# Attention, a gated MLP and a mixer on one core: seven early gelus moved behind the last exp

## The chip, the cores and the metric

One core of one Trainium2 chip runs the whole program, in one launch. The metric is the device time of a run in microseconds (us). The kernel before took 442.62 us, the median of 3 runs (442.54 to 443.59). About 0.3% is what a measurement of this kernel can tell from no change.

Engines by the names of the profile: PE is TensorE's matmul and PEld its weight load, DVE is VectorE, ACT is ScalarE, POOL is GpSimd, SP issues nearly all DMAs. SBUF is the on-chip memory, and PSUM the one into which PE accumulates.

## The reference, cut to what matters

Three layers follow each other. All arrays are float32, with 2 batches, 12 heads, 448 rows of the sequence, 64 numbers per head (768 for all heads), and d_ff = 1024.

```
# attention
scores = q @ k.T / sqrt(64);  scores = cap * tanh(scores / cap)
attn = exp(scores - max) / (sum(exp(scores - max)) + 1e-9);  x = attn @ v

# the gated layer: the change is here
h = gelu(x @ w_in)                      # the tanh form of gelu
u, v = h[..., :512], h[..., 512:]
v_n = (v - mean(v)) / sqrt(var(v) + 1e-6) * g_ln
x = x + (u * (w_sg @ v_n + b_sg)) @ w_out

# the mixer
u = x + (relu(x.T @ w_tok1) @ w_tok2).T
out = u + relu(u @ w_ch1) @ w_ch2
```

## The kernel before, in words

**Attention** runs in twelve steps, one for each pair of heads (pairs 0 to 5 are batch 0, pairs 6 to 11 batch 1). For a pair, PE makes the scores of three blocks of 128 keys, each for both heads, and of the last 64 keys (L540, L655). ACT takes the tanh out of PSUM (L514) and the exp in place (L522). PE then multiplies the weights with the values (L572 for the three blocks, L561 for the last 64 keys), and DVE divides by the sums and splits the result into a high and a low part, `x` (L592 to L616, L351, L367). The step of pair n on PE holds the scores of pair n and the values of pair n-1. Scores lie in PSUM buffers `sc`, values in `gm`, of which there are four.

**Nearly all matrix products** are three matmuls on a high and a low part of each operand (`three`, recorded at L274). The weights arrive as 64-bit numbers. For w_in of v, one ACT pass (L396) and three DVE passes (L438, L449) make a float32 of them, and for the others (w_in of u, w_sg apart, w_out and the mixer's) three ACT passes (L396, L407, L420) and one of DVE (L427). Then the tile is split: cast to the high part, subtraction for the low. The raw tile `r` has two buffers.

**The early units.** When pair 5 is done, x of batch 0 is whole. Its three v units (128 rows each of x @ w_in for v, 18 matmuls of 512 columns) and four u units (128 columns each of u, 18 matmuls of 448) are interleaved with the attention of batch 1. Each ends in a gelu that ACT reads from the unit's `gm` buffer (L768); a v unit goes on with mean and variance on DVE (L814 to L816), a power on POOL (L821), the scaling (L827) and a split into `vn`. After attention come the v units of batch 1, one unit `vr` for the last 64 rows of both batches, the u units of batch 1, then the products with w_sg (`sg_unit`, 11 matmuls each), with w_out, and the mixer.

**The order** is not written out. `Plan` holds every operation with its engines, an estimated duration, a key and what it depends on; `schedule` (L128) repeatedly takes, for each engine, the operation that can start first (the key breaks ties), and the order it finds is emitted engine by engine. The program on the chip keeps this order on every engine and waits only for data and buffers. A dependency that is only in the plan moves instructions and adds no wait. gelu's function is in another table of ACT than tanh and exp, so each change between them is an `ACT_TABLE_LOAD`.

Of the kernel before, what the change touches and what calls it, by code (L numbers as in the profile page):

```python
# [12 lines left out]
AF = mybir.ActivationFunctionType  # L13
# [3 lines left out]
B, H, S, D = 2, 12, 448, 64  # L17
NP = H // 2
DM = H * D
ND = DM // 128  # L20
DF = 512
NF = DF // 128
ST = 112
NS = S // ST
NR = 3
# [197 lines left out]
class Net:  # L223
    def __init__(self, tc, io, pool, ps, anycap=False):
        self.tc, self.nc, self.io, self.pool, self.ps, self.anycap = tc, tc.nc, io, pool, ps, anycap
        self.plan = Plan()
        self.key = 0.0


    def buf(self, tag, shape, dtype=F32):  # L230
# [143 lines left out]
        self.cast(n, hi, src, r, w, key, on or {"ACT": 0}, psum)  # L374
        self.rest(n, lo, src, hi, list(r) + list(w), w, key, rest, psum)

    def weight(self, src, n, key, name):

        nc = self.nc
        rows = src.shape[0]  # L380
        out = self.buf("q" if name in ("wsg", "tok2") else "a", [rows, 2, n], F32R)
        t = self.buf("t", [rows, n], F32 if src.dtype == F32 else I32)
        if src.dtype == F32:
            self.load(rows * n * 4, lambda: nc.sync.dma_start(out=t.ap, in_=src), [t], key=key - 4)
            f = lambda: t.ap
        else:
            raw = self.buf("r", [rows, n, 2], I32)
            self.load(
                rows * n * 8,
                lambda: nc.sync.dma_start(out=raw.ap.rearrange("p n t -> p (n t)"), in_=src.bitcast(I32)),  # L390
                [raw],
                key=key - 4,
            )
            self.act(
                n,
                lambda: nc.scalar.activation(  # L396
                    raw[:, :, 1].bitcast(F32), raw[:, :, 1].bitcast(F32), AF.Copy, scale=2.0**-112
                ),
                [raw],
                [raw],  # L400
                key=key,
            )
            if name in HALVES:

                self.act(
                    n,
                    lambda: nc.scalar.activation(  # L407
                        t.ap.bitcast(U16)[:, 0::2],
                        raw.ap.rearrange("p n t -> p (n t)").bitcast(U16)[:, 1::4],
                        AF.Copy,  # L410
                        scale=2.0**-13,
                        bias=2.0**-14 - 0.5,
                    ),
                    [raw],
                    [t],
                    key=key,
                )
                self.act(
                    n,
                    lambda: nc.scalar.activation(t.ap.bitcast(F16)[:, 1::2], raw[:, :, 1].bitcast(F32), AF.Copy),  # L420
                    [raw],
                    [t],
                    key=key,
                )
                self.dve(
                    n,
                    lambda: nc.vector.scalar_tensor_tensor(  # L427
                        out=t.ap, in0=raw[:, :, 1], scalar=3, in1=t.ap, op0=ALU.logical_shift_left, op1=ALU.bitwise_or
                    ),
                    [raw, t],  # L430
                    [t],
                    key=key,
                    port=True,
                )
            else:
                self.dve(
                    n,
                    lambda: nc.vector.tensor_scalar(  # L438
                        t.ap, raw[:, :, 1], 0x0FFFFFFF, 3, ALU.bitwise_and, ALU.logical_shift_left
                    ),  # L440
                    [raw],
                    [t],
                    fast=2,
                    key=key,
                )
                for half, scalar, op in ((1, -0x80000000, ALU.bitwise_and), (0, 29, ALU.logical_shift_right)):
                    self.dve(
                        n,
                        lambda half=half, scalar=scalar, op=op: nc.vector.scalar_tensor_tensor(  # L449
                            out=t.ap, in0=raw[:, :, half], scalar=scalar, in1=t.ap, op0=op, op1=ALU.bitwise_or  # L450
                        ),
                        [raw, t],
                        [t],
                        key=key,
                        port=True,
                    )
            f = lambda: t.ap.bitcast(F32)
        self.split(n, lambda: out[:, 0], lambda: out[:, 1], f, [t], [out], key, *W_ON[name])
        return out
# [49 lines left out]
    def weigh(self, sc, nn, te, key, dt=0.2):  # L509

        nc = self.nc
        self.act(
            nn * S,
            lambda: nc.scalar.activation(te.ap, sc[:, 0:nn, :S], AF.Tanh, scale=self.qs),  # L514
            [sc, self.cb],
            [te],
            60,
            key,
        )
        self.act(  # L520
            nn * S,
            lambda: nc.scalar.activation(te.ap, te.ap, AF.Exp, scale=self.acap),  # L522
            [te, self.cb],
            [te],
            190,
            key + dt,
        )
# [236 lines left out]
        return x  # L764


    def gelu(self, out, ps, n):
        self.act(n, lambda: self.nc.scalar.activation(out.ap, ps[:, :n], AF.Gelu_apprx_tanh), [ps], [out], 60)  # L768

    def pack(self, x):  # L770

# [25 lines left out]
                psum=psum,  # L797
            )

    def v_unit(self, x, win, si):  # L800

        nc = self.nc
        ps = self.bank()
        cs = slice(0, 128) if si is None else slice(si * 128, (si + 1) * 128)
        terms = []
        for d in range(ND):
            terms += self.three(lambda i, d=d: x[d][:, i, cs], lambda i, d=d: win[d][:, i], [x[d], win[d]])
        self.mm(ps, lambda: ps.ap, terms, 512 / 448)
        v = self.h([128, 512])
        self.gelu(v, ps, 512)  # L810
        st, mv = self.buf("sm", [128, 16]), self.buf("sm", [128, 16])

        def stats():
            nc.vector.bn_stats(out=st[:, 0:6], in_=v.ap)  # L814
            nc.vector.bn_aggr(out=mv[:, 0:2], in_=st[:, 0:6])
            nc.vector.tensor_scalar(mv[:, 1:2], mv[:, 1:2], 1e-6, None, ALU.add)  # L816

        self.dve(800, stats, [v], [st, mv])
        self.gps(
            1700,  # L820
            lambda: nc.gpsimd.tensor_tensor(out=mv[:, 1:2], in0=mv[:, 1:2], in1=self.mhalf, op=ALU.pow),  # L821
            [mv],
            [mv],
        )
        self.dve(
            512,
            lambda: nc.vector.tensor_scalar(v.ap, v.ap, mv[:, 0:1], mv[:, 1:2], ALU.subtract, ALU.mult),  # L827
            [v, mv],
            [v],
            2,  # L830
        )
        vn = self.a([128, 2, 512], F32R)
        if si is None:
            self.halves(512, lambda b, p: vn[p, b], lambda p: v[p], [v], [vn, vn])
        else:
            self.split(512, lambda: vn[:, 0], lambda: vn[:, 1], lambda: v.ap, [v], [vn])
        return vn

    def u_unit(self, x, win, f):
        ps = self.bank()  # L840
        cs = slice(f * 128, (f + 1) * 128)
        terms = []
        for d in range(ND):
            terms += self.three(lambda i, d=d: win[d][:, i, cs], lambda i, d=d: x[d][:, i], [x[d], win[d]])
        self.mm(ps, lambda: ps[:, :S], terms, 1)
        u = self.h([128, S])
        self.gelu(u, ps, S)
        return u

    def sg_unit(self, b, vn, vr, wsg, u, f):  # L850
        nc = self.nc
# [174 lines left out]
    def run(self):  # L1026
        io = self.io
        self.consts()
        rows = lambda t, i, r, c0, n: io[t][i * r : (i + 1) * r, c0 : c0 + n]
        wk = lambda name, k, i: k + KEYS[name][0] + i * KEYS[name][1]  # L1030
        xs = [self.attention_anycap(n) for n in range(B * NP)] if self.anycap else self.attention_all()
        x = [xs[:NP], xs[NP:]]
        k = 10.0 * B * NP + (90 if self.anycap else 13)
        win_v = [self.weight(rows("w_in", d, 128, DF, DF), DF, wk("win_v", 0, d), "win_v") for d in range(ND)]
        win_u = [self.weight(rows("w_in", d, 128, 0, DF), DF, wk("win_u", 0, d), "win_u") for d in range(ND)]

        def stage(units, step):
            nonlocal k
            out = []
            for u in units:  # L1040
                self.key = k
                out.append(u())
                k += step
            return out

        vn, u, g, x2, tr, h1, U = ([None] * B for _ in range(7))
        early, k = (k, k - 70) if self.anycap else (k, EARLY)
        vn[0] = stage([lambda s=s: self.v_unit(x[0], win_v, s) for s in range(NR)], 6.5)
        u[0] = stage([lambda f=f: self.u_unit(x[0], win_u, f) for f in range(NF)], 6.5)
        k = early  # L1050
        vn[1] = stage([lambda s=s: self.v_unit(x[1], win_v, s) for s in range(NR)], 4)
        self.key = k
        xp = self.pack(x)
# [8 lines left out]
        for b in range(B):  # L1062
# [3 lines left out]
            k = kk  # L1066
# [115 lines left out]
```

## Time and profile before

| what | value |
| --- | --- |
| time, median of 3 runs | 442.62 us |
| profiled execution, its own time | 444.11 us |
| span of its trace | 442.3 us |
| mean granted PE clock, share of full | 0.991 |
| PE busy | 427.0 us (97%) |
| ACT busy | 265.7 us (60%) |
| DVE busy | 264.8 us (60%) |
| POOL busy | 105.5 us (24%) |

The profiled execution took 444.11 us, of which the span, from the first instruction to the last, is 442.3 us; 1.81 us lie outside. Its shares are means over stages: from about 40 us to the end of attention at 144.2 us ACT is busy nearly all the time, and after that PE works without a break while ACT has room. So a stretch of the trace tells more than the whole. In the profile, "T idle before, releaser" gives what ended an engine's wait; a matmul's record includes its way through the array, so records of matmuls that follow each other overlap, and the distance between two starts is the better measure of what PE spent.

### The profile page before, as it was taken

How to read it: one execution, taken by the hardware profiler on the slowest of the kernel's cores; microseconds unless marked ns; L12 is line 12 of the kernel's file. 1: busy time of each engine (PE TensorE's matmuls, PEld its weight loads, DVE VectorE, ACT ScalarE, POOL GpSimd, SP SyncE). 2: the span in 40 equal slices, each digit the busy share in tenths (PEclk: the TensorE clock that was granted, in tenths of full speed). 3: DMA queues.
4: the chain of work that ended last, by engine and by line, in shares of the span. 5: the costliest groups of instructions: out<-in, count | busy, mean ns of one | idle time of the engine just before them, and what ended most of it. 6: DMA issues, size and time to landing. Idle time of an engine off the chain costs nothing.

```text
span 442.3 us, 5467 instructions
## 1 busy us (share of the span) xinstructions
PE 427.0 (97%) x2050; PEld 350.2 (79%) x2050; DVE 264.8 (60%) x413; ACT 265.7 (60%) x386; POOL 105.5 (24%) x105
## 2 busy tenths in 40 slices
PE   8997989998999999999999999999999999999994
PEld 5553546566775889999999999999999999999993
DVE  4899989776665765896546899655202242344210
ACT  6998899999999567525537825775404333353100
POOL 0333342320100141567005473111010011011100
PEclk9999989999999999999999999999999999999998
DMA  7535546352120402202402105444201223533010
GB/s 266 207 125 173 176 128 210 102 157 88 47 70 2 142 5 92 83 1 99 139 1 96 48 1 168 164 144 142 96 0 49 96 90 116 184 117 123 34 44 29
DMA packets 14867, 44.84 MB, mean 101 GB/s; under 512 B 1904, under 2 KB 4208, under 8 KB 14832
## 3 DMA queue, kind: packets, MB, share of 16 engines
q1 hardware_dynamic: 14688, 44.30, 30.4%
q8 instruction: 18, 0.29, 0.3%
q14 instruction: 17, 0.14, 0.1%
q10 hardware_dynamic: 144, 0.11, 0.1%
HBM read 41.65 MB, written 2.75 MB: 100 GB/s over the span
## 4 chain that ended last, share of the span: by engine, by line
PE 78%; ACT 12%; DVE 7%; issue 2%; POOL 0%; DVEq 0%; POOLq 0%; ACTq 0%
PE gm L274 48%; PE sc L274 20%; PE gm L572 5%; ACT a L514 3%; ACT a L522 3%; PE sc L540 2%; DVE t L449 1%; DVE q L367 1%; PE sc L905 1%; ACT L768 1%; DVE t L438 1%; DVE h L592 1%; PE gm L561 1%; PE sc L342 1%; DVE h L616 1%
## 5 line engine op out<-in xcount | busy, mean ns | idle before, releaser
L274 PE MATMUL gm<-a,a 128*128 128x448 f32 (+1 forms) x556 | 115.2, 363 | 0.0
L274 PEld LDWEIGHTS gm<-a,a 128*128 128x128 f32 x556 | 102.8, 188 | 8.4
L274 PE MATMUL sc<-x,a 128*128 128x448 f32 x432 | 89.4, 368 | 0.0
L274 PEld LDWEIGHTS sc<-x,a 128*128 128x128 f32 x432 | 81.1, 188 | 8.2
L572 PE MATMUL gm<-a,v 128*128 128x448 f32 x144 | 61.8, 558 | 4.8 <-ACT a L522 2.8
L427 DVE SCALAR_TENSOR_TENSOR t<-r,t 128x512 int32<-128x512 int32 (+1 forms) x52 | 40.5, 782 | 30.1 <-ACT t L420 27.9
L274 PE MATMUL gm<-q,a 128*128 128x448 f32 x268 | 57.3, 367 | 0.0
L407 ACT ACTIVATE t<-r 128x512 uint16<-128x512 uint16 (+1 forms) x52 | 40.5, 784 | 25.3 <-DVE a L367 20.8
L396 ACT ACTIVATE r<-r 128x512 f32<-128x512 f32 (+1 forms) x58 | 38.9, 670 | 25.3 <-DMA r<-ch_in 23.1
L274 PEld LDWEIGHTS gm<-q,a 128*128 128x128 f32 x268 | 50.3, 188 | 4.7
L572 PEld LDWEIGHTS gm<-a,v 128*128 128x128 f32 x144 | 25.5, 191 | 29.6 <-issue 20.6
L368 POOL TENSOR_TENSOR a<-t,a 128x512 fp32r<-128x512 f32 x21 | 29.4, 1402 | 77.6 <-DVE a L351 73.7
L355 POOL TENSOR_SCALAR a<-t 128x512 fp32r<-128x512 f32 x19 | 12.2, 644 | 127.3 <-PE gm L274 71.9
L420 ACT ACTIVATE t<-r 128x512 f16<-128x512 f32 (+1 forms) x52 | 40.3, 774 | 0.0
L367 DVE TENSOR_TENSOR a<-t,a 128x512 fp32r<-128x512 f32 x35 | 24.6, 704 | 20.7 <-POOL a L355 20.1
L522 ACT ACTIVATE a<-a,acap 128x896 f32<-128x896 f32 x36 | 36.5, 1043 | 0.1
L514 ACT ACTIVATE a<-sc,qs 128x896 f32<-128x896 f32 x36 | 35.1, 1004 | 2.2 <-PE sc L540 2.2
L891 POOL TENSOR_TENSOR h<-x 128x448 f32<-128x448 f32 (+1 forms) x25 | 33.5, 1368 | 9.0 <-PE gm L274 6.1
L274 PE MATMUL gm<-x,a 128*128 128x448 f32 x144 | 31.0, 372 | 0.0
L938 DVE SCALAR_TENSOR_TENSOR a<-sc,a 128x896 fp32r<-128x896 f32 x9 | 9.8, 1092 | 33.3 <-ACT a L935 33.3
L274 PEld LDWEIGHTS gm<-x,a 128*128 128x128 f32 x144 | 27.1, 188 | 3.3 <-issue 1.0
L935 ACT ACTIVATE a<-sc 128x896 fp32r<-128x896 f32 x9 | 8.3, 920 | 32.7 <-PE sc L274 32.7
(97 smaller groups left out, 492.5 us busy)
## 6 DMA issues: line engine op xcount, KB each, us to landing
r<-ch_in SPq DMA_DIRECT2D x36, 512.0 KB, 3.3
r<-w_in_in SPq DMA_DIRECT2D x12, 512.0 KB, 3.9
q<-qk_in SPq DMA_DIRECT2D x11, 544.0 KB, 4.3
v<-va_in SPq DMA_DIRECT2D x12, 288.0 KB, 4.4
r<-w_out_in SPq DMA_DIRECT2D x6, 512.0 KB, 3.4
out_t<-h SPq DMA_DIRECT2D x11, 224.0 KB, 1.9
r<-tok_in SPq DMA_DIRECT2D x2, 512.0 KB, 3.4
t<-w_sg_in SPq DMA_DIRECT2D x4, 224.0 KB, 2.5
```

The lines of the kernel that those rows point to most:

```text
L274: self.nc.tensor.matmul(view(), l, rr, start=(i + m == 0), stop=(i + m == n - 1))
L355: lambda: nc.gpsimd.tensor_scalar(out(), src(), 1.0, 0.0, ALU.mult, ALU.add),
L367: "DVE": ("DVE", n / 0.96 + 155, lambda: nc.vector.tensor_tensor(**args()), not psum),
L368: "POOL": ("POOL", n * 2.3 + 60, lambda: nc.gpsimd.tensor_tensor(**args()), True),
L396: lambda: nc.scalar.activation(raw[:, :, 1].bitcast(F32), raw[:, :, 1].bitcast(F32), AF.Copy, scale=2.0**-112),
L407: lambda: nc.scalar.activation(t.ap.bitcast(U16)[:, 0::2], raw.ap.rearrange("p n t -> p (n t)").bitcast(U16)[:, 1::4], AF.Copy, scale=2.0* ...
L420: lambda: nc.scalar.activation(t.ap.bitcast(F16)[:, 1::2], raw[:, :, 1].bitcast(F32), AF.Copy),
L427: lambda: nc.vector.scalar_tensor_tensor(out=t.ap, in0=raw[:, :, 1], scalar=3, in1=t.ap, op0=ALU.logical_shift_left, op1=ALU.bitwise_or),
L514: lambda: nc.scalar.activation(te.ap, sc[:, 0:nn, :S], AF.Tanh, scale=self.qs),
L522: lambda: nc.scalar.activation(te.ap, te.ap, AF.Exp, scale=self.acap),
L572: nc.tensor.matmul(A[h][:, :S], V[:, 3 * j + h : 3 * j + h + 2].rearrange("p c d -> p (c d)"), E[j][:, h], start=(j == 0), stop=(j == 2),)
L891: lambda: self.nc.gpsimd.tensor_tensor(out=out.ap, in0=parts(0), in1=parts(1), op=ALU.add),
```

## The change

The gelu of an early unit no longer stands behind its matmuls. The unit's sums are copied out of PSUM by ACT or DVE, whichever the plan finds free: for v into a buffer `a`, for u into the buffer that holds u afterwards. The gelu, and for v all that follows it, is recorded later, and gelu operations depend in the plan on the last exp, so all fifteen stand behind the whole of attention. The loads of w_in of u depend in the plan on the last exp of the pair with number 6, the seventh pair. The estimate of a gelu's fixed part goes from 60 to 100 ns. The branch of the program for a large cap (`anycap`) keeps its order.

```diff
+        self.last_exp = None
+        self.exps = {}
...
-    def weight(self, src, n, key, name):
+    def weight(self, src, n, key, name, after=None):
...
-            self.load(
+            o = self.load(
                 rows * n * 8,
...
                 key=key - 4,
             )
+            if after:
+
+                o.deps.append(after)
...
-        self.act(
+        self.last_exp = self.exps[int(key // 10)] = self.act(
             nn * S,
             lambda: nc.scalar.activation(te.ap, te.ap, AF.Exp, scale=self.acap),
...
-    def gelu(self, out, ps, n):
-        self.act(n, lambda: self.nc.scalar.activation(out.ap, ps[:, :n], AF.Gelu_apprx_tanh), [ps], [out], 60)
+    def gelu(self, out, src, n):
+        o = self.act(n, lambda: self.nc.scalar.activation(out.ap, src[:, :n], AF.Gelu_apprx_tanh), [src], [out], 100)
+        if self.last_exp:
+
+            o.deps.append(self.last_exp)
...
-    def v_unit(self, x, win, si):
+    def v_unit(self, x, win, si, late=None):
...
         self.mm(ps, lambda: ps.ap, terms, 512 / 448)
+        if late is None:
+            return self.v_rest(ps, si)
+        raw = self.a([128, 512])
+        self.cast(512, lambda: raw.ap, lambda: ps.ap, [ps], [raw], on={"ACT": 0, "DVE": 0}, psum=True)
+        return lambda: self.v_rest(raw, si)
+
+    def v_rest(self, src, si):
+        nc = self.nc
         v = self.h([128, 512])
-        self.gelu(v, ps, 512)
+        self.gelu(v, src, 512)
...
-    def u_unit(self, x, win, f):
+    def u_unit(self, x, win, f, late=None):
...
         u = self.h([128, S])
-        self.gelu(u, ps, S)
-        return u
+        if late is None:
+            self.gelu(u, ps, S)
+            return u
+        self.cast(S, lambda: u.ap, lambda: ps[:, :S], [ps], [u], on={"ACT": 0, "DVE": 0}, psum=True)
+        return lambda: (self.gelu(u, u, S), u)[1]
...
-        win_u = [self.weight(rows("w_in", d, 128, 0, DF), DF, wk("win_u", 0, d), "win_u") for d in range(ND)]
+        win_u = [self.weight(rows("w_in", d, 128, 0, DF), DF, wk("win_u", 0, d), "win_u", self.exps.get(6)) for d in range(ND)]
...
-        vn[0] = stage([lambda s=s: self.v_unit(x[0], win_v, s) for s in range(NR)], 6.5)
-        u[0] = stage([lambda f=f: self.u_unit(x[0], win_u, f) for f in range(NF)], 6.5)
+        late = None if self.anycap else 1
+        vn[0] = stage([lambda s=s: self.v_unit(x[0], win_v, s, late) for s in range(NR)], 6.5)
+        u[0] = stage([lambda f=f: self.u_unit(x[0], win_u, f, late) for f in range(NF)], 6.5)
         k = early
+        if late:
+            self.key = k + 2
+            vn[0] = [f() for f in vn[0]]
+            u[0] = [f() for f in u[0]]
```

On ACT around the scores of pair 8, two gelus of v stand between tables before (L768 is the gelu, `a_889` and `a_893` hold weights of pair 8):

```order
L768 ACT_TABLE_LOAD
L768 ACTIVATE h_877<-gm_817 128x512
L407 ACTIVATE t_880<-r_807 128x512
L514 ACTIVATE a_889<-sc_859,qs 128x896
L514 ACTIVATE a_893<-sc_860,qs 128x896
L350 CAST x_898<-h_875 128x448
L522 ACT_TABLE_LOAD
L522 ACTIVATE a_889<-a_889,acap 128x896
L522 ACTIVATE a_893<-a_893,acap 128x896
L350 CAST a_925<-h_877 128x512
```

and the same place now (L519 is tanh, L527 exp, L401, L412 and L425 are the three passes over a tile of w_in of u, L352 is the copy out of PSUM):

```order
L352 COPY a_845<-gm_788 128x512
L519 ACTIVATE a_851<-sc_829,qs 128x896
L401 ACTIVATE r_810<-r_810 128x512
L519 ACTIVATE a_864<-sc_830,qs 128x896
L412 ACTIVATE t_868<-r_810 128x512
L527 ACTIVATE a_851<-a_851,acap 128x896
L425 ACTIVATE t_868<-r_810 128x512
L527 ACTIVATE a_864<-a_864,acap 128x896
L401 ACTIVATE r_853<-r_853 128x512
L519 ACTIVATE a_899<-sc_872,qs 128x896
L412 ACTIVATE t_916<-r_853 128x512
```

The two table loads and the gelu went; a copy and seven conversion passes of w_in of u, which stood further ahead before, came in.

On ACT at the end of attention, before (`h_1308` is the last exp):

```order
L768 ACT_TABLE_LOAD
L768 ACTIVATE h_1294<-gm_1259 128x448
L514 ACTIVATE a_1300<-sc_1281,qs 128x896
L514 ACTIVATE h_1308<-sc_1296,qs 128x448
L522 ACT_TABLE_LOAD
L522 ACTIVATE a_1300<-a_1300,acap 128x896
L522 ACTIVATE h_1308<-h_1308,acap 128x448
L407 ACTIVATE t_1318<-r_979 128x512
L407 ACTIVATE t_1325<-r_1235 128x512
L420 ACTIVATE t_1318<-r_979 128x512
L350 CAST a_1336<-t_1209 128x512
```

and now (`h_1278` is the last exp, L773 the gelu):

```order
L527 ACTIVATE a_1270<-a_1270,acap 128x896
L527 ACTIVATE h_1278<-h_1278,acap 128x448
L412 ACTIVATE t_1288<-r_1013 128x512
L773 ACT_TABLE_LOAD
L773 ACTIVATE h_1295<-a_776 128x512
L773 ACTIVATE h_1048<-h_1048 128x448
L773 ACTIVATE h_1305<-a_845 128x512
L773 ACTIVATE h_1107<-h_1107 128x448
L773 ACTIVATE h_1317<-a_968 128x512
L773 ACTIVATE h_1185<-h_1185 128x448
L773 ACTIVATE h_1264<-h_1264 128x448
L425 ACTIVATE t_1288<-r_1013 128x512
```

One table load and all seven early gelus now follow the last exp.

On SP, the loads of w_in of u, `r` from `w_in_in`, stand among those of q, k (`q`) and v (`v`), before:

```order
L390 DMA r_501<-w_in_in 128x1024
L503 DMA v_507<-va_in 128x576
L478 DMA q_570<-qk_in 128x1088
L503 DMA v_584<-va_in 128x576
L390 DMA r_613<-w_in_in 128x1024
L390 DMA r_646<-w_in_in 128x1024
L478 DMA q_676<-qk_in 128x1088
L503 DMA v_687<-va_in 128x576
L390 DMA r_709<-w_in_in 128x1024
L478 DMA q_765<-qk_in 128x1088
L390 DMA r_769<-w_in_in 128x1024
L390 DMA r_807<-w_in_in 128x1024
```

and now:

```order
L483 DMA q_657<-qk_in 128x1088
L392 DMA r_663<-w_in_in 128x1024
L392 DMA r_665<-w_in_in 128x1024
L508 DMA v_674<-va_in 128x576
L483 DMA q_739<-qk_in 128x1088
L392 DMA r_774<-w_in_in 128x1024
L508 DMA v_796<-va_in 128x576
L392 DMA r_810<-w_in_in 128x1024
L392 DMA r_853<-w_in_in 128x1024
L483 DMA q_892<-qk_in 128x1088
L392 DMA r_910<-w_in_in 128x1024
```

The first of six comes two pairs' worth of other loads later, behind the q and k of pair 8 (`q_657`), and the last behind those of pair 10 (`q_892`). On PE the order of pairs and units is the same but for details: two v units with pair 7, one with pair 8, two u units with pair 9, and one each with pairs 10 and 11, all seven ahead of the last values of attention.

## Rows read from the trace of the kernel before

**Rows 1.** View of the chain that ended last: share of the span by engine.

```profile
PE 78%; ACT 12%; DVE 7%; issue 2%; POOL 0%; DVEq 0%; POOLq 0%; ACTq 0%
```

**Rows 2.** View by stretches: length, busy time and count per engine, PE clock, DMA.

```profile
52.72:61.84 9.12, 7.16 (x28) 3.55 (x26) 8.89 (x14) 8.55 (x13) 4.35 (x4) 1.00 0.50 151
61.84:65.39 3.55, 3.54 (x15) 2.14 (x15) 2.40 (x5) 3.55 (x6) 0.67 (x1) 0.62 0.44 148
65.39:102.70 37.31, 35.10 (x155) 22.55 (x154) 30.35 (x55) 35.64 (x46) 10.11 (x12) 0.99 0.48 152
102.70:144.20 41.50, 41.01 (x190) 28.05 (x188) 25.36 (x47) 40.31 (x49) 3.63 (x4) 1.00 0.15 46
144.20:177.20 33.00, 33.00 (x155) 28.82 (x154) 22.35 (x42) 21.14 (x34) 7.89 (x9) 1.00 0.26 82
177.20:200.00 22.80, 22.80 (x115) 21.13 (x114) 21.15 (x28) 8.66 (x16) 13.43 (x9) 1.00 0.12 39
```

**Rows 3.** Timeline of PE, 55 to 144 us: start, busy time, line, output<-inputs, count, idle.

```profile
55.82 0.47 PE L540 MATMUL sc<-q 64*128 64x448 f32 x2
...
61.84 1.07 PE L572 MATMUL gm<-a,v 128*128 128x448 f32 x2 [1.42 <-ACT a L522]
...
68.17 0.47 PE L540 MATMUL sc<-q 64*128 64x448 f32 x2
...
83.28 0.47 PE L540 MATMUL sc<-q 64*128 64x448 f32 x2
...
96.96 0.47 PE L540 MATMUL sc<-q 64*128 64x448 f32 x2
...
100.72 2.52 PE L572 MATMUL gm<-a,v 128*128 128x448 f32 x6 [1.32 <-ACT h L768]
...
114.28 0.47 PE L540 MATMUL sc<-q 64*128 64x448 f32 x2
...
121.02 3.81 PE L274 MATMUL gm<-x,a 128*128 128x448 f32 x18
...
124.67 1.66 PE L572 MATMUL gm<-a,v 128*128 128x448 f32 x4
...
126.27 0.48 PE L540 MATMUL sc<-q 64*128 64x448 f32 x2
...
136.68 4.67 PE L572 MATMUL gm<-a,v 128*128 128x448 f32 x12
...
144.20 12.75 PE L274 MATMUL gm<-a,x 128*128 128x512 f32 x54
```

**Rows 4.** Timeline of ACT, 128 to 133 us: a change of tables between tanh and exp.

```profile
128.30 1.90 ACT L514 ACTIVATE a<-sc,qs 128x896 f32<-128x896 f32 x2
130.22 1.28 ACT L522 ACT_TABLE_LOAD   x1
131.52 1.98 ACT L522 ACTIVATE a<-a,acap 128x896 f32<-128x896 f32 x2
```

**Rows 5.** View by lines, whole span: ACT and DVE; count, busy us, mean ns, idle before.

```profile
L768 ACT ACT_TABLE_LOAD x8 | 10.3, 1283 | 0.8 <-PE gm L274 0.7
...
L522 ACT ACT_TABLE_LOAD x7 | 9.0, 1283 | 0.1
...
L768 ACT ACTIVATE h<-gm 128x448 f32<-128x448 f32 (+1 forms) x15 | 8.5, 570 | 7.7 <-PE gm L274 7.6
...
L407 ACT ACTIVATE t<-r 128x512 uint16<-128x512 uint16 (+1 forms) x52 | 40.5, 784 | 25.3 <-DVE a L367 20.8 <-DVE big L1089 4.4
...
L883 DVE TENSOR_TENSOR h<-gm,h 128x448 f32<-128x448 f32 x12 | 7.5, 622 | 8.4 <-PE gm L274 8.3
...
L814 DVE BATCH_NORM_STATS2 sm<-h 128x6 f32<-128x512 f32 x7 | 4.8, 693 | 7.7 <-ACT h L768 7.7
...
L827 DVE TENSOR_SCALAR h<-h,sm 128x512 f32<-128x512 f32 x7 | 4.5, 661 | 0.0
```

**Rows 6.** View of DMA issues: KB each, median us from issue to landing.

```profile
r<-w_in_in SPq DMA_DIRECT2D x12, 512.0 KB, 3.9
```

## The prediction

> **What bounds the kernel now.** I read the chain of waits first: PE holds 78% of it, ACT 12%, DVE 7% [rows 1]. The stretches then say where the 12% lie. From 144.2 us on PE is busy in every microsecond (33.00 of 33.00, then 22.80 of 22.80) while ACT works 21.14 and 8.66 [rows 2]: no ACT time saved there shortens anything. In the four stretches of attention from 52.72 to 144.2 us (91.48 us together) ACT is busy for 8.55 + 3.55 + 35.64 + 40.31 = 88.05 us, and PE shows 1.96 + 0.01 + 2.21 + 0.49 = 4.67 us without a record [rows 2]. So both engines are nearly full there, and the question is which of them gives way when ACT gets lighter. The order on ACT is the same in both kernels up to the first pass over w_in of u, which falls into the step before 55.82, so what comes earlier stays as it is.
>
> The timeline of PE answers it. A step of attention starts with the first of the L540 matmuls of a pair; steps 6 to 11 start at 55.82, 68.17, 83.28, 96.96, 114.28 and 126.27, and attention ends at 144.20 [rows 3]. Step 10 is the cleanest: 11.99 us, in which one u unit takes 124.67 - 121.02 = 3.65 us. What is left, 8.34 us, is what PE needs for a pair alone. A v unit is a third of the 54 matmuls after 144.20, 12.75 / 3 = 4.25 us; a value matmul (L572) is 4.67 / 12 = 0.39 us [rows 3]. With these I set each step against what PE needs for its contents:
> - step 6, a pair alone: 12.35 us against 8.34, 4.0 lost;
> - step 7, two v units, four value matmuls fewer: 15.11 against 8.34 - 1.56 + 8.5 = 15.3, nothing lost;
> - step 8, one v unit: 13.68 against 12.6, 1.1 lost;
> - step 9, two u units: 17.32 against 15.64, 1.7 lost;
> - step 10: the measure itself, 0;
> - step 11, one u unit and the last values (twelve more L572, and six L561 that I put at 0.7 us): 17.93 against 17.4, 0.5 lost.
>
> Together 7.3 us: the most that the change can win before 144.2 us, whatever it takes off ACT. Part of the loss is seen directly: the 4.67 us without a record, and the stretch from 61.84 to 65.39, where the granted clock was 0.62 on average (part of it at 1.2 instead of 2.4 GHz), 3.55 x 0.38 = 1.35 us. The other 1.3 us lie in waits hidden under overlapping records.
>
> **The change part by part.**
>
> Tables. Seven loads before a gelu and seven before the next exp go from attention (fourteen of the fifteen on L768 and L522 [rows 5]; the load for the gelu after attention stays, a little earlier). Each takes 1283 ns, and the neighbours adjoin it: a tanh ends at 130.20, the load runs from 130.22 to 131.50, the exp starts at 131.52 [rows 4]. That is 14 x 1.29 = 18.1 us of ACT. (The Trainium skill, "ScalarE: Activation LUTs", section "What ACT_TABLE_LOAD costs", adds a drain of about 1.38 us to each load, 2.66 us for a switch. By it 14 x 2.66 = 37 us would leave ACT, an estimate. The trace shows 0.02 us between load and exp, no such drain, and the row decides.)
>
> Gelu and copies. Seven gelus of 0.57 us [rows 5], 4.0 us, leave attention, and with them the casts of three normalised v tiles, which I price like a gelu, 0.6 us each. Seven copies out of PSUM come in, four on ACT and three on DVE by the order. No copy out of PSUM of this shape is in the trace. Its nearest rows are the gelu itself, which reads the same buffer (0.57), and DVE's addition from PSUM (0.62) [rows 5]; I take 0.6, so 2.4 us on ACT and 1.8 on DVE. The ends: a copy may find its engine free, and then the `gm` buffer comes free after 0.6 us instead of 1.28 + 0.6, a gain of 1.3 each; or it stands behind a 1 us exp, and nothing is gained. On balance ACT's 88.05 us become 88.05 - 18.1 - 4.0 - 1.8 + 2.4 = 66.5, so ACT is no longer the bound between 55 and 144 us; PE is.
>
> DVE loses mean, variance, scaling and split of three v units in attention, and gains the copies and two or three casts: 30.35 of 37.31 and 25.36 of 41.50 us before [rows 2], so about equal, and not the bound.
>
> Passes over w_in of u. Their number stays, 18 on ACT (L407 is 0.78 us [rows 5], and I take no more than that for the other two) and 6 each of L427, cast and subtraction. They leave steps 5 to 8, where they were spread, for steps 7 to 9. Step 6 gains most: the two idle times I can name there, 1.42 us before 61.84 and the half clock that followed, both stood behind ACT [rows 3]. Step 7 takes it back: by the order ACT does there two pairs of tanh and exp besides three tiles and a copy, about 13 us, inside PE's 15.3; step 8 has about 11.8 inside 12.6. So the passes are covered by the units' own matmuls, with 0.8 us to spare in step 8.
>
> What is then late next, by step: 6 runs with nothing but a pair, so latency between PE, ACT and DVE shows, 0.8; 7, 0.3; 8, 0.6 for the small margin; 9, 0.4, with the wait for the gelu before 100.72 (1.32 us [rows 3]) turned into one for a copy; 10, 0; 11, 0.3, with one table load less ahead of the last exp. Sum 2.4, so 7.3 - 2.4 = 4.9 us are won by the end of attention. The ends of this term: none of the 2.4 remains (7.3 won), or all the losses but the half clock and the waits on gelu remain (2.7 won).
>
> After attention. A table load and seven gelus (1.28 + 7 x 0.6 = 5.5 us) now follow the last exp on ACT, and behind them wait the passes over w_out and w_tok1 and the gelus of batch 1's v units, whose `gm` buffers the u units need. ACT has 33.00 - 21.14 = 11.9 us of idle time up to 177.2, and the first gelu of batch 1 can't start before its 18 matmuls end, 8 us or more after 144.2, so this is covered. On DVE three units' statistics (0.69 for L814 [rows 5] and 0.3 for the two short ones), scaling (0.66) and split (priced like the scaling, 0.7) come in, 2.4 each, 7 us: 22.35 + 7 = 29.4 of 33.00. That fits, narrowly, and the next stretch had DVE at 21.15 of 22.80 already. I charge 0.1 us. If that cover is gone, rival C prices it.
>
> Forecast: 7.3 - 2.4 - 0.1 = 4.8 us. The profiled execution took 444.11 us (442.3 of span and 1.81 around it) and would come to 439.3; it was 1.5 us above the median of the runs, and a time taken now is set against that median: 442.62 - 4.8 = 437.8 us.
>
> **The rivals.**
>
> A, PE runs without any wait from step 6 on: 442.62 - 7.3 = 435.3. For it: step 10 did so with ACT busy nearly all of the time. Against it: steps 8 and 9 wait on three engines in turn, and DVE is busier than in step 10.
>
> B, slower: the tiles of w_in of u come late for the u units. With two `r` buffers a load waits until the tile two before it is combined; it lands 3.9 us after its issue [rows 6], and three ACT passes of up to 0.78 us follow, among tanh and exp in ACT's order. The sixth load stands on SP behind the q and k of pair 10. If load and passes of one tile, 3.9 + 3 x 0.78 = 6.2 us, lie bare before the first u unit, PE stands, and the half clock that followed the idle time of 1.42 us before comes back (1.35): 437.8 + 7.6 = 445.4. It decides from 4.8 us of bare wait on. For it: the passes start about 20 us later than before, and u units don't start later. Against it: by the order the sixth tile is ready 6 to 7 us into step 9, and its six matmuls stand at about 7.5 us there.
>
> The Trainium skill ("TensorE: Matmul & The Clock Gate", section on PSUM-queue depth-cycling) says that short idle times between groups of matmuls, while PSUM banks are cycled, are enough for the clock to drop again and again. Seven copies now stand between unit and bank. By that rule five such places at 1.35 us would cost 6.7 us, and the time would be 437.8 + 6.7 = 444.5, an estimate, on B's side. The trace doesn't bear it out: the stretch with the 1.32 us wait on a bank before 100.72 and that before 144.2 kept 0.99 and 1.00 [rows 2].
>
> C, given back: DVE enters the products with w_sg late, since 29.4 of 33 us leaves 3.6 for all its own waits. Once it is more than the four `gm` buffers behind, PE waits. Half of the 7 us added would be 3.5, less what the buffers hold (about 0.5): 437.8 + 3.0 = 440.8. Against it: the plan put fewer weight passes there, and those can wait.
>
> **How the numbers follow.** The forecast (437.8, its own range 435.8 to 440) has a chance of 0.60, A (435.3) 0.14, C (440.8) 0.14, B (444 to 446) 0.12. The range from 434.6 to 441.6 holds all of the first three and leaves out B and little more. About 0.3%, 1.3 us, is what a measurement of this kernel can tell from no change: faster means below 441.3. The forecast and A lie there with nearly all of their 0.74, C with a third of its 0.14: 0.78. Same is the rest of C and a little of B: 0.10. Slower is B: 0.12.
>
> **What would show it.** Right: no table load between 55 us and the last exp; attention's last value matmul some 5 us earlier, step 6 near 9 us, step 7 unchanged; ACT near 66 us busy over the same steps; PE without a gap after attention; no clock below 1.00 near 60 us. Wrong: a PE wait on a cast or L427 of w_in at the first u unit (B); PE waiting on DVE between the u units of batch 1 and w_out (C); a step 6 still over 11 us would say that ACT wasn't what held it.

## The result and the profile after

| kernel | median, us | runs, us |
| --- | --- | --- |
| before, on the same chip | 442.98 | 442.54 to 443.59 |
| after | 437.12 | 436.68 to 437.26 |

The ratio is 0.9865 [0.9848, 0.9882], so 5.86 us were won (5.2 to 6.7 by the interval); the forecast was 4.8 us and 437.8. The profiled execution of after took 437.02 us with a span of 435.1, against 444.11 and 442.3: 7.1 us. The trace thus shows 1.2 us more than the medians do, and the further profiles of before below say why. Two of the executions of before told below are far off the others, one of 699.11 us (granted clock 0.559) in before_again, which its ratio leaves out, and the profiled one of before_third, 653.48 us (0.37 on average from 300 us on), of which only the first 300 us, at 1.00, are read.

The share of the engines in the chain that ended last, in after, answers to [rows 1]:

```profile
PE 90%; DVE 6%; ACT 3%; issue 1%; POOL 0%; DVEq 0%; POOLq 0%
```

ACT fell from 12% to 3%. The stretches of after by steps 6 to 11 and the two behind attention (columns as in [rows 2]):

```profile
55.58:63.94 8.36, 8.36 (x41) 4.82 (x40) 8.16 (x14) 8.33 (x12) 5.06 (x6) 1.00 0.30 89
63.94:79.79 15.85, 15.85 (x74) 11.15 (x73) 14.76 (x25) 13.66 (x20) 3.88 (x3) 1.00 0.61 201
79.79:92.28 12.49, 12.49 (x59) 8.16 (x58) 10.42 (x19) 11.48 (x16) 2.13 (x2) 1.00 0.56 160
92.28:107.95 15.67, 15.67 (x76) 11.56 (x76) 11.61 (x21) 10.43 (x14) 1.35 (x3) 1.00 0.52 173
107.95:120.02 12.07, 12.07 (x60) 8.16 (x59) 6.98 (x13) 9.31 (x12) 0.95 (x1) 1.00 0.07 19
120.02:137.05 17.03, 17.03 (x76) 10.86 (x76) 11.46 (x24) 12.30 (x17) 1.79 (x2) 1.00 0.09 33
137.05:170.00 32.95, 32.95 (x155) 28.75 (x154) 25.18 (x55) 20.55 (x37) 8.11 (x12) 1.00 0.18 65
170.00:193.00 23.00, 23.00 (x115) 21.32 (x114) 20.75 (x26) 10.28 (x19) 13.58 (x10) 1.00 0.13 43
```

PE's busy time equals the length in every row: it has no idle time in any of them, and the clock is 1.00 in all. ACT sums to 65.51 us of the 81.47 us of the six steps; only in step 6 is it still full. (The 88.05 us of the prediction begin 3.10 us ahead of step 6; with the same 3.10 us of after, where ACT is busy for 1.96, its sum is 67.47.) Against the prediction's price for PE alone (a pair 8.34, a v unit 4.25, a u unit 3.65):

| step | before [rows 3] | after | price of what after has in it |
| --- | --- | --- | --- |
| 6 | 12.35 | 8.36 | 8.34 |
| 7 | 15.11 | 15.85 | 8.34 + 8.5 - 2 x 0.39 = 16.06 |
| 8 | 13.68 | 12.49 | 12.59 |
| 9 | 17.32 | 15.67 | 15.64 |
| 10 | 11.99 | 12.07 | 11.99 |
| 11 | 17.93 | 17.03 | 17.4 |

Step 7 is longer by 0.74 because two value matmuls moved into it from step 5 (8 of them stood in step 7 of before, 10 do now; step 5 became 0.74 shorter, 7.62 against 8.36). Attention ends at 137.05 instead of 144.20, 7.15 us earlier, and from there to the last instruction both kernels take 298.1 us.

The timeline of PE in after (columns as in [rows 3]), at the first u unit, the end of step 9, and the end of attention:

```profile
96.47 2.94 PE L276 MATMUL gm<-x,a 128*128 128x448 f32 x12
...
100.76 1.50 PE L276 MATMUL gm<-x,a 128*128 128x448 f32 x6
...
103.88 4.15 PE L276 MATMUL gm<-x,a 128*128 128x448 f32 x18
107.95 0.47 PE L545 MATMUL sc<-q 64*128 64x448 f32 x2
...
135.79 1.77 PE L577 MATMUL gm<-a,v 128*128 128x448 f32 x4
137.05 12.78 PE L276 MATMUL gm<-a,x 128*128 128x512 f32 x54
```

No row here names a wait. The first u unit began with twelve matmuls at 96.47 and went on with six at 100.76; at this place before had the wait of 1.32 us for a gelu [rows 3]. All waits of PE that the trace of after shows between 30 and 430 us (engine, tile and line, what released it: us in total, times, longest):

```profile
PE gm L577 <- ACT a L527: 1.2, 1, 1.2
PE sc L545 <- DVE q L369: 1.1, 1, 1.1
```

Both lie in step 4, ahead of everything that the change moved:

```profile
39.06 0.67 PE L545 MATMUL sc<-q,q 64*128 64x448 f32 x4 [1.14 <-DVE q L369]
...
43.16 0.99 PE L577 MATMUL gm<-a,v 128*128 128x448 f32 x2 [1.19 <-ACT a L527]
```

ACT in after, at the end of attention, answers to [rows 4]:

```profile
132.06 0.66 ACT L527 ACTIVATE h<-h,acap 128x448 f32<-128x448 f32 x1
132.62 0.77 ACT L412 ACTIVATE t<-r 128x512 uint16<-128x512 uint16 x1
133.39 1.28 ACT L773 ACT_TABLE_LOAD   x1
134.69 0.63 ACT L773 ACTIVATE h<-a 128x512 f32<-128x512 f32 x1
```

It is the one table load left beside that at the start of the program, and the seven late gelus follow it, the first at 134.69, while PE still has attention's last values to do. The copies out of PSUM, which before didn't have (groups by line and shape; count, busy us, mean ns, idle before):

```profile
L353 DVE COPY h<-gm 128x448 f32<-128x448 f32 x2 | 1.2, 625 | 0.5 <-PE gm L276 0.5
...
L352 ACT COPY a<-gm 128x512 f32<-128x512 f32 x2 | 1.2, 587 | 1.3 <-PE gm L276 1.3
L352 ACT COPY h<-gm 128x448 f32<-128x448 f32 x2 | 1.1, 534 | 6.6 <-PE gm L276 6.6
L353 DVE COPY a<-gm 128x512 f32<-128x512 f32 x1 | 0.7, 693 | 0.0
```

Four on ACT, three on DVE, 0.53 to 0.69 us each; 0.6 was assumed.

### The profile page after: what moved, and what is told of

Same layout as the page of the kernel before. It is cut to its first block, busy times and chain, and to the rows that moved or that the text cites. A ratio compares the mean times of both kernels' runs of the same rounds, so it can differ in the third digit from the quotient of the medians.

```text
span 435.1 us, 5461 instructions
## 1 busy us (share of the span) xinstructions
PE 424.8 (98%) x2050; PEld 350.4 (81%) x2050; DVE 267.3 (61%) x422; ACT 248.2 (57%) x375; POOL 99.8 (23%) x100
## 4 chain that ended last, share of the span: by engine, by line
PE 90%; DVE 6%; ACT 3%; issue 1%; POOL 0%; DVEq 0%; POOLq 0%
PE gm L276 52%; PE sc L276 21%; PE gm L577 9%; PE sc L545 4%; PE gm L566 1%; DVE t L454 1%; PE sc L660 1%; DVE q L369 1%; ACT a L519 1%; PE sc L925 1%; ACT a L527 1%; DVE t L443 1%; PE sc L344 1%; DVE h L621 1%; DVE h L597 0%
## 5 line engine op out<-in xcount | busy, mean ns | idle before, releaser
L577 PE MATMUL gm<-a,v 128*128 128x448 f32 x144 | 60.6, 553 | 1.6 <-ACT a L527 1.6
L412 ACT ACTIVATE t<-r 128x512 uint16<-128x512 uint16 (+1 forms) x52 | 40.8, 784 | 24.8 <-DVE a L369 20.5
L401 ACT ACTIVATE r<-r 128x512 f32<-128x512 f32 (+1 forms) x58 | 38.9, 671 | 24.8 <-DMA r<-ch_in 22.2
L370 POOL TENSOR_TENSOR a<-t,a 128x512 fp32r<-128x512 f32 x19 | 25.8, 1359 | 77.7 <-DVE a L353 59.0
L425 ACT ACTIVATE t<-r 128x512 f16<-128x512 f32 (+1 forms) x52 | 40.2, 774 | 0.0
L369 DVE TENSOR_TENSOR a<-t,a 128x512 fp32r<-128x512 f32 x37 | 26.0, 706 | 21.6 <-POOL a L357 20.1
L357 POOL TENSOR_SCALAR a<-t 128x512 fp32r<-128x512 f32 x18 | 11.1, 619 | 119.7 <-PE gm L276 72.0
L519 ACT ACTIVATE a<-sc,qs 128x896 f32<-128x896 f32 x36 | 35.0, 1004 | 5.3 <-PE sc L545 5.3
L527 ACT ACTIVATE a<-a,acap 128x896 f32<-128x896 f32 x36 | 36.5, 1043 | 0.1
```

Of the source, the lines that this page charges most:

```text
L369: "DVE": ("DVE", n / 0.96 + 155, lambda: nc.vector.tensor_tensor(**args()), not psum),
L370: "POOL": ("POOL", n * 2.3 + 60, lambda: nc.gpsimd.tensor_tensor(**args()), True),
L401: lambda: nc.scalar.activation(raw[:, :, 1].bitcast(F32), raw[:, :, 1].bitcast(F32), AF.Copy, scale=2.0**-112),
L412: lambda: nc.scalar.activation(t.ap.bitcast(U16)[:, 0::2], raw.ap.rearrange("p n t -> p (n t)").bitcast(U16)[:, 1::4], AF.Copy, scale=2.0* ...
L577: nc.tensor.matmul(A[h][:, :S], V[:, 3 * j + h : 3 * j + h + 2].rearrange("p c d -> p (c d)"), E[j][:, h], start=(j == 0), stop=(j == 2),)
```

## The experiments

The theory: PE's waits in steps 6, 8, 9 and 11 were the cost, ACT caused them, and each part of the change frees the steps in which its own instructions stood. (The trace of before puts two of these waits down to DVE, 0.61 us in step 8 and 0.19 in step 11, and one to POOL, 0.30 in step 11; same_table tests whether these too hung on ACT.) The readings set against it are named in each expectation. Medians are compared with runs of before on the same chip (443.58 us for the first four kernels, 443.36 for the next four).

**before_again**: the kernel before, unchanged, for the spread and a second profile.

> The kernel before, profiled once more. If the stretch at the half clock near 62 us belongs to every execution, the profile shows it again and the times stay within 0.3% of 443. If it belongs to some executions only (my theory, since the profiled one took 444.1 and the others 442.5 to 443.6), a profile without it has a span near 441 and step 6 near 11 us instead of 12.4; the spread of the times, about 1.3 us, is then this stretch.

443.57 us, ratio 0.9998 [0.9984, 1.0012]. Step 6 took 12.38 us. In its profile the stretch behind the wait of step 6 is again slow (columns as in [rows 2]):

```profile
61.80:65.60 3.80, 3.73 (x14) 2.11 (x14) 2.47 (x5) 3.80 (x7) 0.67 (x1) 0.59 0.48 138
```

**before_third**, the same kernel, for a third look at that stretch:

> One more look at the kernel before. Both profiles of it so far hold a stretch at the half clock in step 6 (12.35 and 12.38 us), while two kernels with the same two waits in step 6 kept the full clock (10.85 us). If the drop hangs on the waits alone, step 6 is 12.4 again; if it comes in some executions only, step 6 may be near 10.9 with the time near 442.1.

Its first 300 us are at full clock, and step 6 took 9.90 us there, with one wait of 1.28 us where the two profiles above have waits of 0.54 and 1.42, or 0.56 and 1.42, and no drop of the clock:

```profile
0.00:300.00 300.00, 291.35 (x1403) 227.91 (x1404) 223.13 (x356) 223.62 (x325) 91.65 (x85) 1.00 0.34 110
300.00:650.00 350.00, 345.45 (x649) 281.82 (x647) 39.94 (x57) 42.09 (x61) 13.78 (x20) 0.37 0.10 33
```

So it is no test of what follows the same two waits.

**before_fourth**, the same kernel again. (The expectation takes the 0.661 of before_third for its whole span; by the rows just shown it was 1.00 up to 300 us.)

> The same look once more, since the one before ran at a clock of 0.661 throughout. Drop tied to the waits: step 6 at 12.4 us. Drop in some executions only: step 6 at 10.9 us and a time near 442.1.

443.61 us in one run, beside 442.58 for before on that chip: not near 442.1, although step 6 took 10.86 us, so the total of one execution doesn't tell whether the drop was there. The timeline of PE from the start of step 6, with the starts of step 7 (67.16) and of what follows attention (143.48), and, below it, the stretch of before_fourth:

```profile
56.30 0.47 PE L540 MATMUL sc<-q 64*128 64x448 f32 x2
...
60.05 0.47 PE L655 MATMUL sc<-q 128*128 128x448 f32 x1 [0.55 <-ACT a L514]
...
62.34 1.02 PE L572 MATMUL gm<-a,v 128*128 128x448 f32 x2 [1.42 <-ACT a L522]
...
67.16 0.47 PE L540 MATMUL sc<-q 64*128 64x448 f32 x2
...
143.48 6.87 PE L274 MATMUL gm<-a,x 128*128 128x512 f32 x28
```

```profile
61.80:65.60 3.80, 3.26 (x17) 1.87 (x18) 3.62 (x7) 3.80 (x7) 0.67 (x1) 1.00 0.44 144
```

The wait of 1.42 us is the one of [rows 3], and the clock stayed at 1.00. So a wait of 1.28 to 1.42 us stands in step 6 of all four profiles of before, and the half clock behind it in two of them; it costs about 12.35 - 10.86 = 1.5 us there. Attention ends at 144.20, 144.21, 142.06 and 143.48 in the four (before, before_again, before_third, before_fourth), so after ends it 7.15, 7.16, 5.01 and 6.43 us earlier; the medians show 5.86 above and 6.31 below.

**gelu_late_only**: the gelus behind attention, w_in of u where it was.

```diff
-  win_u = [self.weight(..., "win_u", self.exps.get(6)) for d in range(ND)]
+  win_u = [self.weight(..., "win_u") for d in range(ND)]
```

> One part alone: gelu of the early units behind attention, w_in of u converted where it was before. Theory 1 (PE's waits end step by step, each edit frees its own steps): step 6, which holds no table load but six or seven passes over w_in of u, stays 2.5 to 4 us above PE's 8.3; steps 8, 9 and 11 go to PE's own time, 3.3 us won, so 439.5. Theory 2 (only the 22 us taken off ACT count, wherever they lie): all is won here, 437.1. Theory 3 (the moved passes carry the gain): nothing won, 442.6.

439.53 us, ratio 0.9912 [0.9891, 0.9933], as theory 1 had it (439.5). Its steps 6, 8 and 9:

```profile
56.34:67.19 10.85, 8.89 (x42) 4.62 (x41) 10.51 (x17) 10.85 (x17) 5.09 (x6) 1.00 0.50 158
...
82.38:94.88 12.50, 12.50 (x60) 8.21 (x59) 9.80 (x19) 10.21 (x14) 2.09 (x2) 1.00 0.57 193
94.88:110.50 15.62, 15.62 (x76) 11.54 (x76) 6.84 (x13) 9.58 (x12) 1.73 (x2) 1.00 0.18 56
```

Steps 8 and 9 are those of after to 0.05 us, and step 11 is (17.05). Step 6 keeps the waits of before, 0.55 and 1.41 us, with ACT busy in all of its 10.85 us: the passes over w_in of u still stand in it. DVE is busy for 10.51 us there too, but ACT has no idle time in which it could have waited for DVE.

**same_table**: before, with tanh in place of gelu in the seven early units. tanh is in the table that exp uses, so the 14 loads go; in the two traces every engine otherwise has the same instructions in the same order. This kernel leaves out the gelu of the seven early units.

```diff
-  def gelu(self, out, ps, n):
+  def gelu(self, out, ps, n, early=False):
+      fn = AF.Tanh if early else AF.Gelu_apprx_tanh
```

> The kernel before in its own order on every engine, but the seven early units take tanh instead of gelu (so the computation is another there), which needs no change of tables: fourteen loads go, and nothing else moves. Theory 1: step 6 unchanged, steps 8, 9 and 11 at PE's own time: 3.3 us won, 439.5. Theory 2: 18 of 22 us go from ACT, so nearly all of the gain, 437.5 to 438. If table loads are no matter at all: 442.6.

439.58 us, ratio 0.9919 [0.9900, 0.9937], the same as gelu_late_only. Steps 6, 8 and 9:

```profile
55.93:66.78 10.85, 8.89 (x41) 4.63 (x41) 10.52 (x17) 10.85 (x17) 5.07 (x6) 1.00 0.50 149
...
81.96:94.45 12.49, 12.49 (x59) 8.16 (x59) 11.26 (x20) 11.00 (x15) 3.12 (x4) 1.00 0.42 137
94.45:110.07 15.62, 15.62 (x76) 11.54 (x76) 10.89 (x20) 10.88 (x15) 2.27 (x3) 1.00 0.32 100
```

The table loads alone carry the whole of what the gelu part of the change brings. Where the gelu itself stands, the copies, and the new estimate of a gelu are worth nothing that these runs can tell. No wait of PE is left behind step 6, so those that the trace of before puts down to DVE and POOL hung on ACT's loads as well. Fourteen loads of 1.29 us, 18.1 us of ACT, bought 4.0 us.

**winu_late_only**: w_in of u behind the seventh pair, gelu where it was.

```diff
-  late = None if self.anycap else 1
+  late = None
   # and gelu() as before, with no dependency on the last exp
```

> The other part alone: w_in of u loaded and converted behind the seventh pair, gelu where it was. Theory 1: step 6 falls to about 8.5 us (2.5 to 4 us won), but its passes now join fourteen table loads in steps 7 to 11, where ACT was busy 73 of 76 us; they add about 4 us there, so in sum -3 + 4: 443.5, between 442 and 445. Theory 2 (sum on ACT): nothing leaves ACT, 442.6. Theory 3 (the moved passes carry the gain): 438 to 439.

442.56 us (12 runs), ratio 0.9978 [0.9966, 0.9990]. Its steps 6 to 9, and two of the waits of PE in steps 8 and 9:

```profile
55.55:63.90 8.35, 8.35 (x42) 4.82 (x41) 8.15 (x14) 8.32 (x12) 5.03 (x6) 1.00 0.30 87
63.90:79.76 15.86, 15.86 (x74) 11.16 (x73) 13.80 (x25) 14.76 (x20) 2.60 (x3) 1.00 0.63 212
79.76:94.08 14.32, 12.73 (x58) 8.09 (x57) 10.46 (x22) 14.26 (x20) 2.77 (x3) 1.00 0.38 108
94.08:112.69 18.61, 16.39 (x78) 11.38 (x77) 14.30 (x28) 18.49 (x25) 3.36 (x4) 1.00 0.49 161
```

```profile
83.79 2.52 PE L577 MATMUL gm<-a,v 128*128 128x448 f32 x6 [1.58 <-ACT h L773]
...
99.02 1.40 PE L577 MATMUL gm<-a,v 128*128 128x448 f32 x3 [1.52 <-ACT h L773]
```

The time alone doesn't decide: theory 1 had expected 443.5, and 442.56 is theory 2's number. The steps do. Step 6 is that of after (8.35). But steps 8 and 9 became 0.64 and 1.29 us longer than before: ACT is busy for 14.26 of 14.32 and 18.49 of 18.61 us, since the passes came on top of tables and gelus, and PE waits for the gelus (and, in step 9, 0.70 us for DVE). The two parts alone bring 4.05 and 1.02 us, 5.1 together; the whole change brings 5.9 and 6.3 (the first result and the next run). Between medians, with their intervals, that difference is at the edge of what can be told. The steps show it plainly: with the passes in them, the tables and gelus cost steps 8 and 9 14.32 - 12.49 and 18.61 - 15.67, 4.8 us together; with the passes further ahead it was 1.2 + 1.7 = 2.9 in before. The passes moved from step 6 lie under PE's work only where the table loads have gone.

**after_again**: the kernel after, with the next three.

> The changed kernel once more, beside the same runs of the kernel before as the next three. Theory 1 (PE's waits in steps 6, 8, 9 and 11 were the whole cost): 437.2, a ratio near 0.986. Of the 7.2 us between the two profiles, 1.4 is the half clock of step 6, which executions of the kernel before have or haven't; if most of them have it, the ratio is nearer 0.985, if few have it, nearer 0.987.

437.05 us, ratio 0.9853 [0.9833, 0.9874]; step lengths as in the table above to 0.02 us.

**extra_act**: after, with nine needless ACT passes of 224 columns in each of steps 9 to 11.

```diff
+  for _ in range(EXTRA if 9 <= n else 0):      # EXTRA = 9
+      o = self.act(224, lambda: nc.scalar.activation(self.scratch.ap, self.bsg[:, 0:224], AF.Copy), ...)
+      o.deps.append(self.last_exp)
```

> The changed kernel with 27 more ACT passes over 224 columns, nine each for pairs 9, 10 and 11, that write a scratch tile nobody reads: some 7.6 us more on ACT in steps 9 to 11, whose 45 us hold 32 us of ACT work. Theory 1 (PE alone sets these steps now): at most 0.6 us slower, 437.2 to 437.8. Theory 2 (ACT's sum still counts): 7.6 us slower, 444.8; half of it, 441, if ACT and PE share the bound.

436.29 us, ratio 0.9841 [0.9825, 0.9857], not slower than after. Steps 9, 10 and 11:

```profile
92.28:107.93 15.65, 15.65 (x78) 11.57 (x77) 11.75 (x20) 13.35 (x22) 2.65 (x3) 1.00 0.51 167
107.93:119.92 11.99, 11.99 (x60) 8.15 (x59) 6.54 (x12) 10.56 (x18) 0.57 (x1) 1.00 0.07 19
119.92:136.95 17.03, 17.03 (x76) 10.88 (x76) 11.56 (x24) 13.82 (x25) 1.79 (x2) 1.00 0.10 33
```

ACT has 37.7 us of work there instead of 32.0, and the steps are as long as without. (By the rows of the passes themselves, 4 of the 27 ran behind these steps, so less was added than the 7.6 us expected.) ACT no longer bounds them: it can take 5.7 us more there at no cost.

**short_units**: after, with the third of the three matmuls left out in the early units, 42 in all.

```diff
-  terms += self.three(...)
+  terms += self.three(...)[: 2 if late else 3]
```

> The changed kernel, with the third of the three products left out in the seven early units (12 matmuls instead of 18, so the low part of one operand is missing from u and v of batch 0): 9.1 us less on PE in steps 7 to 11. Theory 1 (PE sets the steps, ACT next): step 7 becomes ACT's at about 13.9 us, the others shrink by 1.0 to 2.4 us; 7 us faster, 430, between 428 and 432. If DVE or ACT sets these steps already, at most 2 us faster, 435.

428.45 us, ratio 0.9668 [0.9652, 0.9684]: 8.6 us less than after_again. The removed matmuls are a third of three v and four u units, (3 x 4.25 + 4 x 3.65) / 3 = 9.1 us, and the time lies in the expected 428 to 432. Steps 9 and 10, between which a u unit changed places (one now stands in step 9 and two in step 10, the other way round than in after):

```profile
87.72:98.50 10.78, 10.78 (x52) 7.05 (x51) 8.67 (x15) 10.78 (x16) 2.16 (x2) 1.00 0.57 184
98.50:112.35 13.85, 13.36 (x64) 9.21 (x63) 9.64 (x18) 10.60 (x16) 3.38 (x4) 1.00 0.28 87
```

A pair and one short u unit are 8.34 + 2.43 = 10.77 us of PE, a pair and two 13.2. Almost all of PE's time comes back, so PE sets these steps. The first limit behind it shows too: ACT is busy for all of step 9, and step 10 has a wait of 0.49 us for a tanh.

**winv_6_10**: after, with the tiles of w_in of v spread further, so that less of their conversion lies in step 4, where the last waits were. Of the pair of numbers that places the tiles, the second is their distance.

```diff
-  "win_v": (6, 8),
+  "win_v": (6, 10),
```

> The changed kernel with one number changed: the keys of w_in of v are 10 apart instead of 8, one tile for each pair, six pairs long. What is left of waits on PE after the change lies in step 4 (1.14 us before a DVE subtraction of q, 1.19 us before an exp), where DVE is busy 10.8 of 11 us. Theory 1 says that it is DVE's sum there: with the tiles spread, step 4 falls from 10.5 towards 9 us and the time to 435.7. If the wait comes from the load of q or from ACT, or the last tile is late for the first v unit in step 7: 437.2 or more.

434.85 us (434.73 to 435.04), ratio 0.9809 [0.9794, 0.9825], which beats both kernels: 2.2 us under after_again, and the two intervals don't meet. Step 4 takes 8.35 us instead of 10.52, with DVE busy for 7.97 instead of 10.29. Since matmuls move between the steps behind it, steps 4 to 7 together tell what was won: 40.30 us instead of 42.35. Step 4, and below it all waits of PE between 11 and 430 us:

```profile
37.35:45.70 8.35, 8.35 (x40) 4.80 (x39) 7.97 (x15) 8.35 (x12) 1.40 (x2) 1.00 0.40 114
```

```profile
PE sc L545 <- ACT a L519: 0.5, 1, 0.5
PE gm L577 <- ACT a L527: 0.2, 1, 0.2
```

## Why the prediction was right

**The bound.** That PE is the bound once ACT is lighter, and that a step's worth is its length less PE's price of its contents, held: the six steps of after stand within 0.4 us of their prices, and extra_act and short_units show both sides of it. ACT came to 67.47 us over the prediction's stretch (88.05 before), where 66.5 was worked out.

**The term that was mis-sized** is the charge of 2.4 us for "what is then late next, by step". It measured nothing: PE has no wait from step 6 on. Step 6 was charged 0.8 for latency between PE, ACT and DVE and has 0.02; steps 8 and 9, charged 0.6 and 0.4, are at their price. Step 7 did become longer, by 0.74, but by two matmuls that left step 5, not by a wait. ACT is full in step 6 (8.33 of 8.36) and PE has no wait there all the same: a full engine beside the bound had been charged as if it must cost something.

**What kept the forecast near** is an error the other way. The 7.3 us that the change could win before 144.2 were taken from one execution, with 1.35 us for the half clock of step 6 in them, and set against the median of the runs. The four profiles of before show that this loss (1.5 us by the two lengths of step 6) comes in some executions only. Against these four profiles after wins 7.15, 7.16, 5.01 and 6.43 us, and a gain of 5.9 to 6.3 between medians lies among them; how often the half clock comes in executions that weren't profiled is not shown. The prediction's 4.8 was too small by 1.1 us, less than the 2.4 charged in error, because 7.3 was too much. That two errors of opposite sign left 437.8 within 0.7 us of 437.12 is luck; that PE would bound the steps is not.

**After attention**, 0.1 us was charged and nothing was lost. The seven gelus lie at 134.69 to 138.2, and DVE has 25.18 of 32.95 us, less than the 29.4 feared. (The text beside the listings around pair 8 counts two gelus and seven passes; the listings hold one gelu and five passes. No term of the sum rests on these counts.)

**The rivals.** A, PE without any wait from step 6 on, is what the trace shows, so the mechanism that came true is the one that had a chance of 0.14. Its 435.3 wasn't reached, for the reason just told. B, w_in of u late: the last tile did make ACT wait 1.27 us for its DMA at 94.24, and both parts of the first u unit still began with no wait. C, DVE late for the products with w_sg: no wait.

The rule from the Trainium skill ("TensorE: Matmul & The Clock Gate", section on PSUM-queue depth-cycling) is that short idle times while PSUM banks are cycled drop the clock again and again. After has no wait of PE from step 6 on, so its granted clock of 1.00 in every stretch shown is no test of that rule. The waits that the runs do have point both ways: behind those of 1.14 and 1.19 us in step 4 of after the clock stayed at 1.00, and behind the one of 1.42 us in step 6 of before it was 0.62, 0.59 and 1.00 in three profiles.

The drain that the Trainium skill ("ScalarE: Activation LUTs", section "What ACT_TABLE_LOAD costs") adds to each load isn't seen: with 37 us less, an estimate from the page's figure, ACT would have had 88.05 - 37 - 3.4 = 47.7 us, and it has 67.47.

**The signs named ahead**: no table load between 55 us and the last exp (held); last value matmul some 5 us earlier (7.15); step 6 near 9 us (8.36); step 7 unchanged (0.74 longer); ACT near 66 (67.5 over the same stretch); no gap after attention (held); no clock under 1.00 near 60 us (held).

## What to carry to other kernels

Price each step by what the engine that should bound it needs for its contents, taken from a step without waits; the difference is all that lighter work on another engine can win, here 7 us by the profiles for some 20 us taken off ACT. Two changes that load the same engine must be priced together: moving passes off one full step pays only where the other change has made room. And a loss that stands in one profile, such as a stretch at half clock, needs a second profile of the same kernel before it goes into a sum that is set against a median.

## What the runs showed of the hardware

- The granted clock in the stretch behind the same wait of 1.42 us in step 6 was 0.62 and 0.59 on average in two profiles of before and 1.00 in before_fourth; gelu_late_only and same_table, with waits of 0.55 and 1.41 there, kept 1.00, and so did before_third with 1.28. What decides it stays open.
- A copy of float32 out of PSUM took 0.53 us (448 columns) and 0.59 us (512) on ACT, 0.63 and 0.69 on DVE: about as much as a gelu out of PSUM (0.57 on average [rows 5]). So a copy on ACT in place of a gelu saved nothing there but the table.
